# An early query bound over eight key tiles instead of four, with another order of the tasks

## The chip, the core and the metric

The kernel runs on one core of a Trainium2 chip. Five engines of that core take part: PE (TensorE: matmuls, and PEld, its weight loads), ACT (ScalarE), DVE (VectorE), POOL (GpSimd) and SP (SyncE, which here only issues DMAs). Each engine takes its instructions strictly in its own order and waits on semaphores that the others raise. The metric is the device time of the core in microseconds; lower is better. Three runs of the kernel before gave 791.34, 791.4 and 791.9 us, a median of 791.4 us.

## The reference

`x` has 2048 rows of 640 numbers in bf16. It is layer-normed once, and two branches read it: attention with 32 heads of 20 dimensions over all 2048 positions, and a two-stage MLP mixer whose result gates the attention's.

```python
def reference(A_x, A_wqkv, A_wo, B_x, B_w1, B_w2, B_w3, B_w4):
    ...
    # _A_ref: attention
    qkv = (x @ wqkv).reshape(B, S, 3, H, Dh).transpose(2, 0, 3, 1, 4)
    q, k, v = qkv[0], qkv[1], qkv[2]
    scores = jnp.einsum("bhqd,bhkd->bhqk", q, k) * (Dh ** -0.5)
    p = _softmax(scores, axis=-1)
    o = jnp.einsum("bhqk,bhkd->bhqd", p, v)
    ... @ wo
    # _B_ref: h = gelu(layernorm(x) @ w1), shifted by rows, @ w2; x1 = x + that;
    #         x1 + gelu(layernorm(x1) @ w3) @ w4
    ...
    x = A_x
    xn = _layernorm(x, axis=-1)
    s = _A_ref(xn, A_wqkv, A_wo)
    g = _silu(_B_ref(xn, B_w1, B_w2, B_w3, B_w4))
    return x + s * g
```

## The kernel before

**Tiling.** The 2048 positions are 16 key tiles of 128 and 4 query chunks of 512 (`NQC`). The 32 heads go in 8 quads of 4. For each quad and each query chunk (32 groups, named `quad_qc`, the first is `0_0`) the kernel makes, for every key tile, the scores of four heads (`sc`, lines 1615 and 1632), their exponentials, and the product with V (`pv`, line 1424). One ACT instruction (`exp`, line 1684) takes the scores of two heads of one key tile, 128 by 1024. Part of the exponentials is made by DVE from bit patterns (line 1707 and the additions of line 1594, or on POOL line 1592) for four key tiles of a group, in two blocks of two (`BLK`); these are the "units". Everything else is put between as it fits: projections of the next quads, the whole mixer branch, the output projection (all line 725).

**The shift under the exponent.** So that the exponentials stay in range, every query gets a shift computed from a bound: the largest absolute key component (`MXc[:, c]`, line 1209, one number for each of the four key chunks `c`, made from the product `KT_c`) times the sum of the absolute query components. The final bound (`mq_`, line 1226) needs all four key chunks. To start sooner, group `0_0` first uses an *early* bound, made by `early()` from the first key chunk alone (`mqe`, `she`, `qade`, lines 1178, 1184, 1188). Its queries (`qe`) serve the first `EARLY` = 4 key tiles; after these, `between()` (`fs`, `fe`) makes the factor by which the sums so far are rescaled (`rescale`), and the remaining tiles use the final bound (`sh_0`, `qad_0`, lines 1157 and 1163).

**The start.** The tiles of x come by eight DMAs of two tiles each (`ld_x`, line 912); the weights of the first quad (`ld_wp`, line 1094) and the V weights of the first half (`ld_wv0`, line 1333) come by three more on the same queue. Layer norm of the 16 tiles: for those in `LNV` DVE takes the statistics (`bn`, line 936); for those in `LNS` (tiles 1, 4, 5, 14, 15) ACT sums x and x squared (`sx`, `sxx`, lines 982 and 984). The normed tiles are transposed, by PE for chunks 0, 1 and 3 (`tr_x`, line 1071; copied out of PSUM by ACT, line 1079, or DVE, line 1082) and by DMA for chunk 2 (line 1060). Then come the products `QT_c` and `KT_c` (queries and keys of the first quad) and `v0_n` (V), each of five steps over the 640 inputs, each step four matmuls side by side. The first step of such a product waits for all five pieces of its transposed input. `kev_c` (line 1212, ACT) copies the keys out after `mx_c`.

**The order.** No engine chooses at run time: `TABLE`, a string at the end of the file, lists all 6715 tasks in one order and names the PSUM bank or buffer that each takes; `Planner.follow` reads it and derives the semaphores. The TensorE work before the first data are `NPF[0]` = 36 warm-up groups (`warm`, line 899). `AGAIN` names score matmuls that are issued more than once.

In the order of before, the starts are as follows (read from `TABLE`):

```
SP : ld_x0 ld_x2 ld_x4 ld_x6 ld_wp_1 ld_x8 ld_x12 ld_wp_0 ld_x14 ld_wv0 ld_x10 | tx_9 tx_8 ...
ACT: sx1 sxx1 sx4 sxx4 sx5 norm1 sxx5 trev_x0 (3) sx14 norm4 norm5 sxx14 qev_0 trev_x1 (5)
     sx15 kev_0 sxx15 exp (5) kev_1 trev_x3_3 exp (2) kev_2 kev_3 exp exp exp fe exp ...
PE : warm (21) tr_x0 and warm ... KT_0_0 QT_0_0 KT_0_1 QT_0_1 v0_0 (4) KT_0_2 ... she ... KT_1
```

Of the kernel before, what the change touches and what calls it, by code (L numbers as in the profile page):

```python
# [464 lines left out]
class Handle:  # L465
    _n = 0
# [11 lines left out]
class Cfg:  # L478
# [5 lines left out]
    def __init__(self, S=2048, D=640, H=32, F=1536):  # L484
# [60 lines left out]
        self.NPF = [36, 0]  # L545
# [39 lines left out]
        self.AGAIN = {(2, 2, 4, 2): 2, (7, 0, 1, 0): 1, (7, 0, 1, 1): 1, (7, 0, 8, 2): 2, (7, 1, 5, 0): 1, (7, 1, 6, 2): 1, (7, 1, 7, 3): 1, (7, 1, 9, 0): 1, (7, 1, 12, 0): 1}  # L585
        self.EARLY = 4
        self.ND = ([2, 4, 4, 4],) + tuple([5, 4, 5, 4] for _ in range(5)) + ([5, 5, 5, 5], [5, 5, 4, 4])
        self.PP |= {(quad, qc, 0, 2) for quad in range(8) for qc in range(4)}
        self.PP |= {(0, 0, 1, 3), (0, 0, 1, 2)}


    def order(self, quad, qc):
# [4 lines left out]
        first = 0 if quad + qc else 1  # L597
# [51 lines left out]
class Gen:  # L649
# [196 lines left out]
    def alloc_persistent(self):  # L846
# [44 lines left out]
        for k in range(cfg.NPF[0]):  # L891
            T("pe", 427 if k < 14 else 216, self.warm, reads=[A("Ob")], writes=[("PV", 0)], name=f"warm{k}")
# [204 lines left out]
    def prep(self):  # L1097
# [74 lines left out]
        def early():  # L1172
            e0 = self.e4[:, :]
            T("pool", 250, lambda e: e.memset(QE[:, 1536:1664], 0.0), writes=[A("mqe")], name="mqe0")
            for k in range(2):
                T("pool", 250, lambda e, k=k: e.tensor_scalar(sel[:, k, :, :], bass.AP(e0.tensor, e0.offset, [list(e0.ap[0]), [1, 4], [0, 32]]), 2.0 * k - 1.0, None,
                                                              op0=ALU.mult), reads=[A("e4")], writes=[A("sel", k)], name=f"sel{k}")
            T("dve", 90, lambda e: e.tensor_scalar(mqe[:, :, 20], self.maskn[:, 0:4], MXc[:, 0:1], None, op0=ALU.mult),
              reads=[A("MXc", 0), A("maskn"), A("mqe")], writes=[A("mqe")], name="mqe", lock=True)
# [22 lines left out]
        for c in range(NQC):  # L1202
            if c == 1:
                early()
# [929 lines left out]
    r"#9#6#:#;#<#=#>#?#@#A#B#C###_#p#,$O#(#{#`#a$P$d#-#)$8#%#&#'#*#.#$#+#j#k#i#4#D#l#u&V$N#q&W#m#E#F#G#H#I#J#n#t#r$R#v#s$Q#2#w$S#o#b$$#g$W$T#x#K#c#}#|#L$##M#N$p%$u"  # L2134
    r"'#O#P%(#$U#~$%#z#Q#R#S#T#U$&$X$Y$Z$V#y#V#W#X$z)${$|#e$}%)%*%+#Y$v%#$$]$[$~%,$/$+$,$'%$%%$-$q%&$^#Z$w$x#[$r$s$*#h#f$_&U$y$e%'$t$0$`#]#^#d%k)%d(%l%e&X#$a$b&Y&Z"
    r"&[%m%f%2$$c%g%7'%n$(%h$E$)%r%<&%3$f&]%i%=$.%>$H$1$=$2%o$3%-%%8%4%5%9%.%/%6$G%0&g(&h%?&i%1%@$C#0&`$%:&j&a&b&c%A%&d%B$<$9$6$7$:%p%;$>$;%u%j$?$4%C%D&n&&o$I&^%v#"
    r"$D&e&k$F$@%w%E$5$J&p&q&r$A&s&{$%x%&l$g%q%y&|%z%{&}&~'#*.#*?&*@'*/$%|'%('&'''($h'$#/$K$B$i$j',$*A%%G$M$k')'-$l*0''*'.$L$m*<&*=''/$n&:($o*8#*9$'0'1*>)&;&<%}*C&"
    r"*D'&=%O$*:#&>*E(%~%J&%P%K%T'%U&?*B%V%L%Q%R%S%W%M%Y#%Z%[%X%]%^%_(%`%a%b%F%H%I&#)&$%t'2(K&m%s&%&&%c*5%%N*G'*F(*6$&*$*H$&+&'&,&-&.'?#&L%'@&M(L&(&/'A*7)&)&0(M&1&"
    r"2'B'C'D(N'+*1#*2$&6)&N&O&P*3&&C#&D&7*O&*L#*N%*M$*P%&Q*b)*Q*a(*;&E&F&G&8&*c#*4&H+(%+'$&9&@+)'*T(*U)*W*Y'*Z&*I'M&*[&'N'O'P'Q*J*S$*R%&A$'R&u%&v*]&*^'&B&w&x#5'i'"
    r"h&3&y+2#*V)+3$'3('4'5'6'7*X*_$&z*e&+4(*d'*k#+$(+%)*j$'8*`'9(':';'<'=*m*f)*o'*n&+&&*g*p$'>*r$*q#*K(P+T'E&_*s*i)*h('F('G'H+6&+5'&I'I'J'K*l%+*+D)+C(+<$&R+=#*v'Y"  # L2140
    r"('Z'[+7#'L']'^'S#'T'_+E)+>&+8+/)+.(+9&+#'U+0(*|'V'W+:%+X$+;%+W#+,('X++)'a#'b+Z'c'd'e'f+K%+J&+_#+-$+^$+?&J#+G(+L#+H)*w*t+a+U%+l$+V&+m#&K+o+I%*~*y*x+Y&(O,&','("
    r"&S$&T+M,('+1+r#+s$,*%,)&*u*}+['+](,+$+u'j$'k+x+@%,E#(T&t+A&+`#,D$+B%'l'm'n*{,F('o*z'p#+F+d(+c)+N+e),7&,6%'q'r+g#,9+f$'s+b+p(+q)'t+O'u,,,4%,5&+h%,<#,=$,?+t#,8"
    r"$'`2h+~+{+i+j'+k('v$&4'w'x+n&,B&,:#,A%,;$'y'z'|#'}'~,C)(#,R%,>%'{,I(,H),Q&,T($(%,J'+z,@,o$,p#,q$,%(U,K)-&,W&(&,L(,X%,Z,$(',M#+w,k$,h',l#,G,#+y,m%,i&+v+}-4(-5"
    r")(Q&,[(R(S(e,j)-6&-)&,w%(^(V(z-*',v$,x(/y+|,n,-)-,,.(,U'-/&-0%,0$,1#,/),],N,2%,V(+P,Y#,d-2'g()$(*(+,3,r#,s$,y%,z&,f,t),^(,,e(-,a,_-=#,{%->$,P',O(,u,c-(%-'&(."
# [128 lines left out]
```

## Time and profile before

| what | us |
|---|---|
| median of the runs | 791.4 |
| the profiled execution | 791.33 |
| its span on the core | 789.6 |
| ACT busy | 760.5 |
| PE busy (pipelined, an upper bound) | 774.8 |
| DVE busy | 704.1 |
| POOL busy | 441.7 |
| first exponential starts | 22.41 |
| ACT runs without a gap from | 36.13 |
| last exponential ends | 782.6 |

The span is the time from the core's first instruction to its last; 1.7 us lie around it. Rows of the profile name a line of the kernel, the engine, the operation and its shapes, a count, busy time and the mean length in ns, and after the bar the idle time of the engine just before and what ended it. A timeline row has the start, the length and what ran; a row with x5 is five instructions without a gap. Lengths of pipelined instructions overlap: the next may start before the last one's end.

### The profile page before, as it was taken

To read this page: it belongs to the slowest core of one execution; us is meant where nothing else is said; L and a number is where in the kernel's file an instruction comes from. 1 tells how busy PE (TensorE), PEld (TensorE's weight loads), DVE (VectorE), ACT (ScalarE), POOL (GpSimd) and SP (SyncE) were. 2 spreads that over 40 slices of the span, in tenths; PEclk is the share of its full clock that TensorE was granted. 3 is DMA by queue.
4 is the path that set the end of the run, shared out by engine and by line. 5 is a ranking of instruction groups with operands and counts; after the bars stand their busy time and mean duration, and the time that the engine had idled before them with its cause. 6 is when DMAs were issued, how large, how long until landed. Compare 5 with 4: busy or idle time off the path is not lost.

```text
span 789.6 us, 27717 instructions
## 1 busy us (share of the span) xinstructions
PE 774.8 (98%) x12461; PEld 294.0 (37%) x12461; DVE 704.1 (89%) x936; ACT 760.5 (96%) x791; POOL 441.7 (56%) x238
## 2 busy tenths in 40 slices
PE   9999999999999999999999999999999999999997
PEld 5432333334434333333433333333334333333454
DVE  8888889889999999989998889898989899897987
ACT  7999999999999999999999999999999999999896
POOL 5666556562556647665564654656544546536733
PEclk9999999999999999999999999999999999999999
DMA  5332433253111233524233222234331123114343
GB/s 174 48 99 87 102 87 100 57 132 68 39 36 37 47 71 70 85 55 94 54 74 74 43 75 48 61 70 77 74 96 29 36 43 87 20 17 136 93 145 102
DMA packets 141349, 58.09 MB, mean 74 GB/s; under 512 B 113728, under 2 KB 136432, under 8 KB 141232
## 3 DMA queue, kind: packets, MB, share of 16 engines
q1 hardware_dynamic: 141232, 56.33, 30.8%
q8 instruction: 97, 1.59, 0.9%
q14 instruction: 20, 0.16, 0.1%
HBM read 34.70 MB, written 10.33 MB: 57 GB/s over the span
## 4 chain that ended last, share of the span: by engine, by line
PE 67%; ACT 26%; DVE 6%; issue 0%
PE psum L725 23%; ACT arena L1684 22%; PE psum L1615 19%; PE psum L1606 12%; PE psum L1424 8%; DVE arena L1707 3%; PE psum L899 1%; ACT arena L2090 1%; PE psum L1632 1%; ACT arena L1998 1%; PE psum L1481 1%; ACT arena L1661 1%; ACT arena L2118 1%; DVE arena L1594 1%; PE psum L1455 1%; PE psum L1071 0%
## 5 line engine op out<-in xcount | busy, mean ns | idle before, releaser
L1684 ACT ACTIVATE arena<-psum 128x1024 bf16<-128x1024 f32 x718 | 671.6, 1041 | 17.0 <-PE psum L1615 12.6
L1592 POOL TENSOR_TENSOR arena<-arena 128x2048 int32<-128x2048 int32 x92 | 330.1, 3599 | 207.8 <-DVE arena L1594 91.7
L1707 DVE TENSOR_SCALAR arena<-psum 128x1024 uint16<-128x1024 f32 x276 | 335.6, 1221 | 47.9 <-PE psum L1615 44.4
L725 PE MATMUL psum<-arena 128*32 128x320 bf16 (+1 forms) x5808 | 335.0, 333 | 0.2
L1615 PE MATMUL psum<-arena 32*128 32x512 bf16 x1935 | 257.7, 384 | 6.5 <-ACT arena L1684 2.7
L1606 PE MATMUL psum<-arena 128*22 128x512 bf16 x2208 | 193.0, 381 | 0.3 <-DVE arena L1594 0.3
L725 PEld LDWEIGHTS psum<-arena 128*32 128x32 bf16 x5808 | 137.4, 96 | 120.4 <-issue 50.6
L1615 PEld LDWEIGHTS psum<-arena 32*128 32x128 bf16 x1935 | 69.2, 91 | 227.8 <-ACT arena L1684 133.4
L1594 DVE TENSOR_SCALAR arena<-arena 128x4096 uint16<-128x4096 uint16 (+1 forms) x139 | 141.4, 1038 | 1.7 <-PE psum L1606 0.8
L1424 PE MATMUL psum<-arena 128*22 128x512 bf16 x1432 | 135.2, 382 | 0.0
L1606 PEld LDWEIGHTS psum<-arena 128*22 128x22 bf16 x2208 | 49.5, 90 | 65.8 <-issue 43.7
L1741 POOL TENSOR_TENSOR arena<-arena 128x512 bf16<-128x512 f32 x30 | 40.7, 1355 | 41.7 <-DVE arena L1594 26.7
L1424 PEld LDWEIGHTS psum<-arena 128*22 128x22 bf16 x1432 | 34.0, 90 | 49.2 <-issue 28.6
L2083 DVE CAST arena<-psum 128x512 bf16<-128x512 f32 x48 | 32.8, 685 | 4.8 <-PE psum L725 4.5
L1291 DVE CAST arena<-psum 128x512 bf16<-128x512 f32 x40 | 27.1, 685 | 2.9 <-PE psum L725 2.6
L1906 POOL TENSOR_TENSOR arena<-arena 128x640 bf16<-128x640 bf16 x12 | 17.1, 1436 | 21.1 <-DVE arena L1840 9.0
L936 DVE BATCH_NORM_STATS2 arena<-arena 128x6 f32<-128x320 bf16 x54 | 24.7, 477 | 1.6 <-POOL arena L980 1.4
L1661 ACT ACTIVATE arena<-psum 128x2048 bf16<-128x2048 f32 x13 | 24.6, 1889 | 0.7 <-PE psum L1615 0.6
L953 POOL TENSOR_SCALAR arena<-arena 128x640 bf16<-128x640 bf16 x16 | 13.9, 875 | 19.2 <-DVE arena L1594 14.2
L1632 PE MATMUL psum<-arena 128*32 128x512 bf16 x240 | 23.4, 381 | 0.1
L1728 DVE STREAM_TRANSPOSE arena<-psum 128x512 f32<-128x512 f32 x30 | 21.3, 712 | 1.6 <-PE psum L1606 1.0
L1840 DVE SCALAR_TENSOR_TENSOR arena<-psum,arena 128x320 bf16<-128x320 f32 x32 | 15.3, 488 | 6.8 <-PE psum L725 6.3
(135 smaller groups left out, 338.1 us busy)
## 6 DMA issues: line engine op xcount, KB each, us to landing
arena<-in_B_w_dram SPq DMA_DIRECT2D x48, 160.0 KB, 2.8
arena<-arena SPq DMA_DIRECT2D x124, 32.0 KB, 1.9
arena<-in_B_w_dram SPq DMA_DIRECT2D x4, 960.0 KB, 5.3
arena<-in_A_x_dram SPq DMA_DIRECT2D x8, 320.0 KB, 5.6
arena<-in_A_x_dram SPq DMA_DIRECT2D x16, 160.0 KB, 2.6
out_dram<-arena SPq DMA_DIRECT2D x16, 160.0 KB, 1.8
heads<-arena SPq DMA_DIRECT2D x120, 20.0 KB, 2.0
arena<-keys SPq DMA_DIRECT2D x28, 80.0 KB
```

The lines of the kernel that those rows point to most:

```text
L725: ins = e.matmul(pb[32 * c:32 * c + 32, 0:N], lhsT(k, c), rhs(k, c), start=(k == 0), stop=(stop and k == nk - 1), tile_position=(0, 32 * c))
L1424: ins = e.matmul(pb[32 * i:32 * i + 22, 0:512], VA[:, ql, kts[i // 2], i, :], PT[:, slots[i // 2][0].slot, slots[i // 2][0].at(i % 2):slot ...
L1592: return e.tensor_tensor(dst.bitcast(I32), U[:, ub, 0:w].bitcast(I32), bass.AP(c.tensor, c.offset, [list(c.ap[0]), [0, w // 2]]), op=ALU.add)
L1594: fa if onp else lambda e, v=v, dst=dst: e.tensor_scalar(dst, U[:, ub, 0:w], EXP_B[v], None, op0=ALU.add),
L1606: ins = e.matmul(pb[32 * i:32 * i + 22, 0:512], wv, dst[:, at:at + 512].bitcast(BF16), start=first, stop=final, tile_position=(0, 32 * i))
L1615: return e.matmul(out, self.KT[32 * i:32 * i + 32, b, 128 * kt:128 * kt + 128], q, start=True, stop=True, tile_position=(32 * i, 0))
L1632: ins = e.matmul(out[32 * c:32 * c + 32, :], self.KT[:, b, 128 * kt + 32 * c:128 * kt + 32 * c + 32], self.QM[:, gb, i, :], start=True, st ...
L1661: lambda e: e.activation(self.PT[:, hp[0].slot:hp[0].slot + 2, :], self.psum[:, 512 * h0.slot:512 * h0.slot + 2048].rearrange("p (a b) -> ...
L1684: lambda e: e.activation(self.PT[:, hp.slot, :].rearrange("p (a b) -> p a b", b=512), self.banks(hs), AF.Exp, scale=cfg.scale),
L1707: return e.tensor_scalar(U[:, ub, 1024 * at:1024 * at + 1024].rearrange("p (a b) -> p a b", b=512), self.banks(hd), a_exp, EXP_BIAS, op0=A ...
L1741: return e.tensor_tensor(OnT.rearrange("p (k d a) -> p a k d", k=4, a=4), Ob[:, :].rearrange("p (a k d) -> p a k d", a=4, k=4), in1, op=AL ...
L2083: T("dve", c_dve(512), lambda e, h=h, fc=fc, i=i, G=G: e.tensor_copy(G[:, i, fc, :], self.wbank(h)[:, 0:512]), reads=[wa], writes=at, name ...
```

## The change

- `EARLY` goes from 4 to 8: in group `0_0` the first eight key tiles (0 to 7) use the early bound. `early()` is now built after `KT_1` instead of `KT_0`, and a new DVE instruction (`mqm`) with a changed `mqe` takes the larger of the first two chunks' maxima.
- With it the two blocks that DVE serves in `0_0` become tiles (10, 11) and (14, 15) instead of (6, 7) and (10, 11); the POOL additions of that unit stay two.
- Tiles 14 and 15 move from `LNS` to `LNV`: DVE takes their statistics, and four ACT instructions (`sx14`, `sxx14`, `sx15`, `sxx15`) go. POOL applies the norm to them in both versions.
- Four warm-up groups fewer. `AGAIN` has 22 repeats instead of 11.
- `TABLE` is another: another order on all engines, above all in the first 60 us, and other PSUM banks.

```diff
-        self.NPF = [36, 0]
+        self.NPF = [32, 0]
...
-        self.AGAIN = {(2, 2, 4, 2): 2, (7, 0, 1, 0): 1, (7, 0, 1, 1): 1, (7, 0, 8, 2): 2, (7, 1, 5, 0): 1, (7, 1, 6, 2): 1, (7, 1, 7, 3): 1, (7, 1, 9, 0): 1, (7, 1, 12, 0): 1}
-        self.EARLY = 4
+        self.AGAIN = {(0, 1, 2, 2): 1, (0, 1, 5, 3): 1, (0, 1, 6, 2): 1, (5, 2, 2, 0): 1, (5, 2, 2, 1): 1, (6, 2, 12, 3): 1, (7, 0, 1, 2): 3, (7, 1, 2, 0): 2, (7, 1, 2, 1): 2, (7, 1, 6, 0): 1, (7, 1, 6, 1): 1, (7, 1, 7, 2): 2, (7, 1, 7, 3): 2, (7, 1, 8, 3): 3}
+        self.EARLY = 8
+        self.LNV = self.LNV + [[14, 15]]
+        self.LNS = [[1], [4, 5]]
...
-        self.PP |= {(0, 0, 1, 3), (0, 0, 1, 2)}
+        self.PP |= {(0, 0, 2, 3), (0, 0, 2, 2)}
...
-        first = 0 if quad + qc else 1
+        first = 0 if quad + qc else 2
...
-            T("dve", 90, lambda e: e.tensor_scalar(mqe[:, :, 20], self.maskn[:, 0:4], MXc[:, 0:1], None, op0=ALU.mult),
-              reads=[A("MXc", 0), A("maskn"), A("mqe")], writes=[A("mqe")], name="mqe", lock=True)
+            M2, m2 = self.RZ[:, 1, 0:4], A("RZ", 1)
+            T("dve", 90, lambda e: e.tensor_scalar(M2, self.maskn[:, 0:4], MXc[:, 0:1], None, op0=ALU.mult), reads=[A("MXc", 0), A("maskn")],
+              writes=[m2], name="mqm", lock=True)
+            T("dve", 90, lambda e: e.scalar_tensor_tensor(mqe[:, :, 20], self.maskn[:, 0:4], MXc[:, 1:2], M2, op0=ALU.mult, op1=ALU.min),
+              reads=[A("MXc", 1), A("maskn"), A("mqe"), m2], writes=[A("mqe")], name="mqe", lock=True)
...
         for c in range(NQC):
-            if c == 1:
+            if c == cfg.EARLY // 4:
                 early()
...
 TABLE = (
...
```

The starts in the new order:

```
SP : ld_x0 ld_x2 ld_x4 ld_x6 ld_wp_1 ld_x10 ld_x8 ld_wp_0 ld_x14 ld_x12 ld_wv0 | tx_9 tx_8 ...
ACT: sx1 sxx1 sx4 sxx4 sx5 norm1 sxx5 trev_x0 (3) norm4 norm5 qev_0 trev_x1 (5)
     kev_0 kev_1 exp (7) trev_x3_3 exp (2) kev_2 exp exp kev_3 exp ...
PE : warm (24) tr_x0 and warm ... QT_0_0 v0_0 (4) QT_0_1 QT_0_2 QT_0_3 v0_2_0 QT_0_4 v0_2 tr_x1 ...
     KT_0 (5) KT_1 (5) ... she ... sc
```

Past the first 110 of ACT's tasks its order differs from the old one only in some 25 places, by a few tasks each.

More of the change, by code (lines that the diff above doesn't have):

```diff
@@ L891, in alloc_persistent @@
         for k in range(cfg.NPF[0]):
-            T("pe", 427 if k < 14 else 216, self.warm, reads=[A("Ob")], writes=[("PV", 0)], name=f"warm{k}")
+            T("pe", (427 if k < 14 else 216) + 900 * (k == 0), self.warm, reads=[A("Ob")], writes=[("PV", 0)], name=f"warm{k}")
         self.step = 0
@@ L2237 @@
[L2237 to L2238 removed]
+    r"#6#9#:#;#<#=#>#?#@#A#B#C#D##&T#E#F#l#G#H#I#J#K#L#M#N#O#%#,#-#&#'#$#w#(#0#*#+#)#Z#g#.#f&U$X#e#[#]#h#m#i$W#P#Q#q#^#p#j#n#k$Y#r#o$Z$[#c#s#2$]$^#y#x#`#{$|(#z#|#t"
+    r"$_#u#_#}#v#~$+$a$,$4$b$c$#$)$d#R#S$`#T$r$%%#$f$}$m&#d$n$o$p$e$g#b#a$$$-$s%&$h$t$u$i$~%#$q%'$v&S%(%)$w%%$$($x(I$j#U#V$y$z#W$8$*$O${$'$k$%$A$.#X#Y$&%a'&V$&W&X&"
```

208 lines of the change are left out of this document (103 added, 105 removed).

## The prediction

> **What bounds the kernel now.** First the page: the busy time of each engine and ACT's largest group.
>
> ```profile
> span 789.6 us, 27717 instructions
> PE 774.8 (98%) x12461; PEld 294.0 (37%) x12461; DVE 704.1 (89%) x936; ACT 760.5 (96%) x791; POOL 441.7 (56%) x238
> ...
> L1684 ACT ACTIVATE arena<-psum 128x1024 bf16<-128x1024 f32 x718 | 671.6, 1041 | 17.0 <-PE psum L1615 12.6
> ```
>
> PE and ACT both look full, so the second view is the busy time by stretches, and the third the waits of ACT behind the start (36 to 782 us).
>
> ```profile
> 14.00:24.00 10.00, 9.99 (x287) 6.92 (x278) 9.81 (x39) 9.64 (x19) 5.62 (x11) 1.00 0.34 55
> 24.00:36.00 12.00, 11.99 (x254) 5.54 (x254) 9.63 (x22) 10.63 (x14) 7.17 (x10) 1.00 0.19 18
> 36.00:60.00 24.00, 23.66 (x368) 8.36 (x364) 20.96 (x29) 23.93 (x27) 17.36 (x14) 1.00 0.33 95
> ...
> ACT arena L1684 <- PE psum L1615: 11.0, 27, 0.7
> ACT arena L1684 <- PE psum L1481: 1.8, 5, 0.5
> ACT arena L1684 <- PE psum L1424: 1.2, 2, 0.8
> ```
>
> The columns of a stretch are its length, then PE, PEld, DVE, ACT, POOL busy. From 36 to 60 us ACT is busy 23.93 of 24 us while PE issues 15 matmuls per us; from 14 to 24 it issues 29. So PE has room behind the start, and ACT sets the pace there; its waits in 746 us sum to 14.6 (the three rows and 0.6 more). Before 36 us ACT waits: that is where the change acts. The timeline of ACT in that stretch:
>
> ```profile
> 13.49 0.73 ACT L982 ACTIVATE arena<-arena 128x640 bf16<-128x640 bf16 x1
> 15.89 0.72 ACT L984 ACTIVATE arena<-arena 128x640 bf16<-128x640 bf16 x1
> 16.68 0.69 ACT L1145 ACTIVATE arena<-psum,arena 128x512 bf16<-128x512 f32 x1
> 17.49 2.59 ACT L1079 ACTIVATE arena<-psum 128x512 bf16<-128x512 bf16 x5
> 21.36 0.73 ACT L984 ACTIVATE arena<-arena 128x640 bf16<-128x640 bf16 x1
> 22.41 4.69 ACT L1684 ACTIVATE arena<-psum 128x1024 bf16<-128x1024 f32 x5 [0.23 <-PE psum L1615]
> 26.95 0.81 ACT L1212 ACTIVATE arena<-psum,arena 128x512 bf16<-128x512 f32 x1
> 27.62 0.62 ACT L1079 ACTIVATE arena<-psum 128x512 bf16<-128x512 bf16 x1
> 29.07 1.94 ACT L1684 ACTIVATE arena<-psum 128x1024 bf16<-128x1024 f32 x2 [0.83 <-PE psum L1615]
> 30.90 1.45 ACT L1212 ACTIVATE arena<-psum,arena 128x512 bf16<-128x512 f32 x2
> 33.80 1.94 ACT L1684 ACTIVATE arena<-psum 128x1024 bf16<-128x1024 f32 x2 [0.55 <-PE psum L1615]
> 36.13 24.25 ACT L1684 ACTIVATE arena<-psum 128x1024 bf16<-128x1024 f32 x26
> ```
>
> The first exp starts at 22.41; from 36.13 the exps run solid, 24.25 us for 26, about 0.92 each. Whatever the change gains or loses by the point of equal work at 36.13, the rest carries to the end. In between ACT has 12.2 us of work (10 exps at 0.91, from 4.54 for five, `kev_1` 0.67, the copy 0.62, `kev_2` and `kev_3` 1.32, `fe` 0.5) and 1.5 us of waits.
>
> **The change part by part.** *Four sums less on ACT.* The row of 15.89 is followed at 16.68: 0.79 for a sum with the reading of its result, 3.1 us for the four (two more rows are those of 13.49 and 21.36), all ahead of the first exp. That is the largest gain on offer, if ACT's next instruction is ready.
>
> *It waits for another.* The new order gives x12 the tenth place of SP's queue and the V weights the last. The rows of the queue and of the two landings:
>
> ```profile
> 7.00 0.68 SPq L1333 DMA_DIRECT2D arena<-in_A_wqkv_dram  x1
> 7.73 0.94 SPq L912 DMA_DIRECT2D arena<-in_A_x_dram  x1
> ...
> arena<-in_A_wqkv_dram SPq DMA_DIRECT2D x1, 400.0 KB, 6.9
> arena<-in_A_x_dram SPq DMA_DIRECT2D x1, 320.0 KB, 7.0
> ```
>
> The tenth load lands at 7.00 + 6.9 = 13.9, the eleventh at 7.73 + 7.0 = 14.7. In the old order x10 is last and PE waits for nothing there (busy 9.99 of 10 us from 14 on). In the new one `v0_0`, which reads the V weights, stands in PE's queue between `QT_0_0` and `QT_0_1`. PE waits there until 14.8, and behind it `QT_0`, the x1 transposes, `KT_0`, `KT_1`, so `qev_0` and everything on ACT after it. (Fewer warm-ups let the first transposes go some 0.75 us earlier; this wait swallows it.) Rows for what follows:
>
> ```profile
> 9.77 1.90 PE L899 MATMUL psum<-arena 128*32 128x512 bf16 x32
> 16.78 0.39 PE L725 MATMUL psum<-arena 128*32 128x512 bf16 x3
> 18.34 0.71 PE L725 MATMUL psum<-arena 128*32 128x320 bf16 x16
> 19.52 0.39 PE L1184 MATMUL psum<-arena 128*32 128x512 bf16 x4
> 21.93 0.40 PE L1615 MATMUL psum<-arena 32*128 32x512 bf16 x4
> ...
> 10.44 1.28 DVE L936 BATCH_NORM_STATS2 arena<-arena 128x6 f32<-128x320 bf16 x3
> 17.26 0.69 DVE L1209 TENSOR_REDUCE arena<-psum 128x1 f32<-128x512 f32 x1
> 18.05 0.18 DVE L1178 TENSOR_SCALAR arena<-arena 128x4 bf16<-128x4 f32 x1
> 19.96 0.75 DVE L1188 SCALAR_TENSOR_TENSOR arena<-psum,arena 128x512 bf16<-128x512 f32 x1
> 27.23 1.42 DVE L1082 COPY arena<-psum 128x512 bf16<-128x512 bf16 x4
> 31.36 0.24 DVE L1226 TENSOR_SCALAR arena<-arena 128x4 bf16<-128x4 f32 x1
> 32.27 0.75 DVE L1163 SCALAR_TENSOR_TENSOR arena<-psum,arena 128x512 bf16<-128x512 f32 x1 [0.23 <-PE psum L1157]
> ```
>
> A step of four 512-column matmuls takes 0.217 (1.90 less 0.38 for the tail, over seven), one of 320 columns 0.137, and a product can be read 0.48 after its last step starts (16.78 to 17.26). From 14.8: `v0_0` four steps 0.55, `QT_0_1` to `_3` 0.65, `v0_2_0` 0.14, so `QT_0_4` starts at 16.14 and `qev_0` at 16.6, as before (16.68). Three more V steps and the x1 transposes put the five copies at 17.3 to 19.9 (0.5 apart, as in the row of 17.49). So ACT is where it was, with 1.55 of the four sums gone into idling.
>
> *The early bound over two chunks.* The old chain reaches `qade` from `KT_0` alone, at 19.96. The new one needs `KT_1`, whose first step waits for the last x1 copy: 20.05, five steps 1.08, readable at 21.4; `mx_1` 0.65, a small one 0.1, `mqe` 0.2, `she` after 0.15 and readable in 0.44, `qade` 0.75: 23.7; score 0.15 later, exp 0.48 after it (21.93 to 22.41): first exp at 24.35, 1.9 us later than now. `mqm` (priced as `mqe`, 0.1 to 0.2) runs while DVE waits and costs nothing. The other 1.5 us of the removed sums also become waiting; what is kept is `kev_1` done ahead (0.67).
>
> *DVE.* The two tiles add four statistics (0.4 apart in the row of 10.44) and some 0.45 of small ones, about 2.1 us. Ahead of `mx_0` they are covered: `aq_0` in DVE's queue waits for `qev_0` until 17.4, three statistics and small ones bring DVE to `mx_0` by 19.2, and `KT_0` is readable only at 19.9. Without that cover they would delay the chain one for one. Behind `qade` the norm of tiles 12 and 13 ends DVE's next 16 instructions (5.8 us by their rows' kinds) at 29.6, so the x3 transposes, and the eighth exp that PE has behind them, come at about 31.75, where ACT is free at 31.25: a wait of 0.5.
>
> *More early tiles.* Fourteen exps, not eight, go before the final bound is needed, so the two old waits (0.83 and 0.55 in the rows, 1.5 with their edges) go. Late next is the final bound itself: with the x3 copies at 30.8 instead of 27.23 `mq_` comes at 34.9 (now 31.36) and `qad_0`, 0.9 behind it and 0.75 long, ends at 36.4. The first exp on it is due at 39, but its score `sc0_0_10_1` stands in PE's queue ahead of the early `sc0_0_6_1y`, whose exp is due at 37.6 and can start at 37.45. It just fits.
>
> Sum at equal work: 24.35 + 11.55 (12.2 without `kev_1`) + 0.5 = 36.4, against 36.13: 0.3 lost.
>
> *POOL and SP past the start.* POOL's norms of tiles 14 and 15 wait for DVE's small results about as long as now; `ld_w1`, `kt0`, `qt0` and `qm0`, which change places, have their readers in later groups, and POOL is busy only 56% of the time: nothing on the path. Without that cover a late `qm0` would hold up the first group that reads it by as much as it is late. *`AGAIN`* adds 11 score matmuls, 2.4 us of PE at 0.217, at places where PE has room behind 36 us; without the room all 2.4 would count. *Four warm-ups fewer* save 0.87 us of PE ahead of data: nothing.
>
> *The rest of the order.* ACT has the same work behind the start; of its 34 waits (0.42 each) a re-ordering can remove or add a few. No row shows which; I bound it by three of them either way, 1.3 us. The scores stand in 558 runs of row matmuls instead of 566. The chain of waits shows a single pair:
>
> ```profile
> 37.41 0.32 PE psum L1615 x2
> ```
>
> This is 0.1 above a step's 0.217, so eight runs less are 0.8 us of PE. A third of it where ACT waits: 0.3 gained.
>
> Total: 791.33 (the profiled execution: span 789.6 and 1.7 around it; the median of the runs is 0.07 above) + 0.3 - 0.3 = 791.3 us. No change, by the bound of 0.2% (1.6 us), which is about what a measurement of this kernel can tell from none.
>
> **The rivals.** *It helps.* If the V weights land by 13.3, `qev_0` follows the norm of tile 5 at about 15, the last x1 copy ends at 18.4, and the first exp comes 1.4 earlier, at 22.95, where DVE's queue is the next limit. With the wait of 0.5 at the eighth exp gone too and 0.3 from the rest: 791.33 + 0.3 - 1.4 - 0.5 - 0.3 = 789.4. For it: ACT's 3.1 us are truly gone. Against: the landings came in order of issue, and total bytes are the same.
>
> *It hurts: the final bound comes late and early scores queue behind it.* Place: `sc0_0_10_1` ahead of `sc0_0_6_1y` on PE. The slack is 0.15 us; each us by which DVE's x3 copies, `KT_3`, `mx_3` or `mq_` slip further is one us of ACT. From a slip of 2 us (DVE's added 2.1 us uncovered) it decides: 791.3 + 1.85 = 793.2. For it: DVE is busy 9.81 of 10 us from 14 to 24. Against: its queue idles at `aq_0` and `mx_0` in my count.
>
> *The clock falls.* PE idles in the new start some 1.5 us for the V weights and again before `she`. The weight-load rows at the kernel's start, where each group is one of the warm-ups:
>
> ```profile
> 6.94 0.16 PEld L899 LDWEIGHTS psum<-arena 128*32 128x32 bf16 x4 [0.26 <-issue]
> 7.36 1.48 PEld L899 LDWEIGHTS psum<-arena 128*32 128x32 bf16 x28 [0.26 <-issue]
> ```
>
> Groups come 0.42 apart until 7.36 and 0.21 apart after it: PE runs at half rate for its first 5.5 us. Should it fall back in the start, which PE's issue fills, 2.75 us of matmuls are lost: 794.1. The Trainium skill ("TensorE: Matmul & The Clock Gate", Part 1) says that the clock is halved after an idle window of about 3.4 us. By that rule two shorter idles don't trigger it, and the time stays at 791.3; the rows above show the slow beginning, and none here shows a fall after it.
>
> **How the numbers follow.** No change (including that the removed work is only turned into waiting) 0.45, between 789.8 and 792.9. It helps 0.33, around 789.4 and down to 788.4 if two or three waits of ACT behind the start go as well. It hurts 0.19, around 793.2, and the clock 0.03, 794.1. Leaving out the lowest of the first and the upper ends of the others, 788.8 to 793.6 holds 8 in 10. Faster 0.33, same 0.45, slower 0.22.
>
> **What would show it.** Right: PE idle until 14.7 or so behind the first step of `QT_0`, `qev_0` near 16.6, the first exp near 24.35, ACT idling about 3 us between its x1 copies and that exp, then solid with at most one wait of 0.5 until 37. The Wv step is wrong if line 725 runs 320-column matmuls before 14; the chain is wrong if the first exp comes before 23. The forecast falls if ACT's waits behind 40 us differ from 14.6 by more than 1.6, or if ACT waits at the sixth tile for line 1163.

## The result and the profile after

| | before | after |
|---|---|---|
| median of 21 runs, us | 791.25 | 792.88 |
| lowest to highest, us | 790.61 to 792.55 | 792.10 to 795.74 |
| profiled execution, its span, us | 791.33, 789.6 | 792.68, 791.0 |

The change makes the kernel slower: the ratio of the times is 1.0024, with a 95% interval of 1.0018 to 1.0030, so 1.4 to 2.4 us. The prediction of 791.3 us and no change was wrong; its range holds the time.

The page of the kernel after, the busy times and ACT's largest group:

```profile
span 791.0 us, 27621 instructions
...
PE 775.0 (98%) x12420; PEld 292.9 (37%) x12420; DVE 706.4 (89%) x942; ACT 758.3 (96%) x783; POOL 440.8 (56%) x238
...
L1689 ACT ACTIVATE arena<-psum 128x1024 bf16<-128x1024 f32 x718 | 672.0, 1039 | 19.2 <-PE psum L1620 14.3
```

ACT has 2.2 us less to do (758.3 against 760.5), yet its exps idle 2.2 us more (19.2 against 17.0). Line numbers are two or five higher than before, by where the change adds lines: the exp of line 1684 is 1689, the scores of 1615 are 1620, the products of 725 are 727.

Busy times by stretches (the length, then PE, PEld, DVE, ACT, POOL), and ACT's waits from 36 to 782 us:

```profile
14.00:24.00 10.00, 9.84 (x268) 5.60 (x264) 9.18 (x31) 6.78 (x11) 4.27 (x11) 1.00 0.19 37
24.00:36.00 12.00, 12.00 (x264) 5.56 (x252) 10.06 (x29) 11.50 (x14) 6.60 (x10) 1.00 0.44 69
36.00:60.00 24.00, 22.97 (x354) 9.03 (x355) 19.43 (x26) 21.56 (x24) 16.77 (x15) 1.00 0.15 42
```

```profile
ACT arena L1689 <- PE psum L1620: 12.6, 32, 0.9
ACT arena L1689 <- PE psum L1486: 1.8, 4, 0.7
ACT arena L1689 <- PE psum L1429: 1.2, 2, 0.8
```

Up to 36 us the new kernel does well: from 24 to 36 ACT is busy 11.50 of 12 us, where before it was 10.63. From 36 to 60 it falls to 21.56 of 24, where before it was 23.93. The waits behind 36 us sum to 16.7 us (the three rows and 1.1 more), 2.1 above the 14.6 before. Where they lie shows in the timeline of ACT:

```profile
15.43 0.69 ACT L1147 ACTIVATE arena<-psum,arena 128x512 bf16<-128x512 f32 x1 [0.61 <-PE psum L727]
...
22.83 6.68 ACT L1689 ACTIVATE arena<-psum 128x1024 bf16<-128x1024 f32 x7 [1.28 <-PE psum L1620]
...
30.59 1.94 ACT L1689 ACTIVATE arena<-psum 128x1024 bf16<-128x1024 f32 x2 [0.48 <-PE psum L1620]
...
35.58 6.52 ACT L1689 ACTIVATE arena<-psum 128x1024 bf16<-128x1024 f32 x7
41.98 0.60 ACT L1205 ACTIVATE arena<-psum 128x512 f32<-128x512 f32 x1
43.01 2.86 ACT L1689 ACTIVATE arena<-psum 128x1024 bf16<-128x1024 f32 x3 [0.42 <-PE psum L1620]
46.37 1.94 ACT L1689 ACTIVATE arena<-psum 128x1024 bf16<-128x1024 f32 x2 [0.51 <-PE psum L1620]
48.91 3.83 ACT L1689 ACTIVATE arena<-psum 128x1024 bf16<-128x1024 f32 x4 [0.60 <-PE psum L1620]
53.22 1.94 ACT L1689 ACTIVATE arena<-psum 128x1024 bf16<-128x1024 f32 x2 [0.49 <-PE psum L1620]
55.59 7.44 ACT L1689 ACTIVATE arena<-psum 128x1024 bf16<-128x1024 f32 x8 [0.43 <-PE psum L1620]
```

Eleven exps are done by 35.58, and the 18th ends at 42.10. Before, ten were done by 36.13, at 0.93 each the 18th ended at about 43.6, and `fe`, 0.5 us, lay ahead of it, which here comes behind it, at 41.98. So at 42 us ACT is about 1.0 us ahead. Then five waits of 0.42 to 0.60, 2.45 in sum, fall between 43 and 56 us, where before there is none. The 36th exp starts at 59.34 before and at 61.02 after: the lead of 1.0 has become a lag of 1.7. At the end 1.4 of it is left.

The chain of waits says who holds ACT there: the kernel after, pieces from 37 us on.

```profile
37.52 2.75 ACT arena L1689 x3
...
40.32 0.68 PE psum L1620 x4
...
42.88 1.34 PE psum L727 x36
44.22 0.32 PE psum L1620 x2
44.54 1.19 PE psum L727 x20
...
46.31 1.74 PE psum L727 x48
...
55.02 0.55 PE psum L1620 x3
...
55.59 1.95 ACT arena L1689 x2
```

And the kernel before:

```profile
40.50 0.37 PE psum L1615 x2
...
40.89 7.45 ACT arena L1684 x8
...
48.38 0.39 PE psum L1615 x2
```

Before, ACT itself is the chain from 40.89 to 48.34. After, PE is, without a break from 40.32 to 55.57: V products and Q products (line 727), with one or two pairs of scores between them now and then. From 42 to 56 us no row of PE shows a wait (it is busy 13.82 of 14 us), while each of ACT's five waits is ended by a score of PE. ACT's early lead was scores that PE had issued ahead of these products; the products remained.

### The profile page after: what moved, and what is told of

The parts are those of the page before. It is cut to its first block, busy times and chain, and to the rows that moved or that the text cites. A ratio compares the mean times of both kernels' runs of the same rounds, so it can differ in the third digit from the quotient of the medians.

```text
span 791.0 us, 27621 instructions
## 1 busy us (share of the span) xinstructions
PE 775.0 (98%) x12420; PEld 292.9 (37%) x12420; DVE 706.4 (89%) x942; ACT 758.3 (96%) x783; POOL 440.8 (56%) x238
## 4 chain that ended last, share of the span: by engine, by line
PE 74%; ACT 19%; DVE 3%; SPq 2%; DMA 1%; issue 0%; POOL 0%; POOLq 0%
PE psum L727 27%; PE psum L1620 22%; ACT arena L1689 16%; PE psum L1611 13%; PE psum L1429 9%; ACT arena L2095 1%; PE psum L1637 1%; DVE arena L1712 1%; DMA arena<-in_A_wqkv_dram 1%; SPq L914 1%; PE psum L1486 1%; DMA heads<-arena 0%; ACT arena L2123 0%; SPq L1387 0%; PE psum L1460 0%
## 5 line engine op out<-in xcount | busy, mean ns | idle before, releaser
L1689 ACT ACTIVATE arena<-psum 128x1024 bf16<-128x1024 f32 x718 | 672.0, 1039 | 19.2 <-PE psum L1620 14.3
L727 PE MATMUL psum<-arena 128*32 128x320 bf16 (+1 forms) x5808 | 329.3, 333 | 0.7 <-DMA arena<-in_A_wqkv_dram 0.3
L1620 PE MATMUL psum<-arena 32*128 32x512 bf16 x1946 | 261.2, 384 | 6.3 <-ACT arena L1689 3.3
L727 PEld LDWEIGHTS psum<-arena 128*32 128x32 bf16 x5808 | 135.5, 96 | 121.1 <-issue 48.6
L1911 POOL TENSOR_TENSOR arena<-arena 128x640 bf16<-128x640 bf16 x12 | 16.7, 1398 | 22.0 <-DVE arena L1845 10.4
```

The lines of the kernel that those rows point to most:

```text
L727: ins = e.matmul(pb[32 * c:32 * c + 32, 0:N], lhsT(k, c), rhs(k, c), start=(k == 0), stop=(stop and k == nk - 1), tile_position=(0, 32 * c))
L1620: return e.matmul(out, self.KT[32 * i:32 * i + 32, b, 128 * kt:128 * kt + 128], q, start=True, stop=True, tile_position=(32 * i, 0))
L1689: lambda e: e.activation(self.PT[:, hp.slot, :].rearrange("p (a b) -> p a b", b=512), self.banks(hs), AF.Exp, scale=cfg.scale),
```

## The experiments

Three theories stand in the expectations. *A* is the prediction's: behind the start ACT sets the pace and PE has room, so the loss must come from the start. *P*: between about 41 and 55 us PE's queue sets the pace, so work and order on PE count there. *Q*: the masked copies of Q for the second group (`qm0_1`), which come late in the new order, hold up the first scores of that group and what stands behind them.

All results in one table. The difference is that of the medians to the kernel before on the same chip; the two columns behind it are from the profiles: the start of the first exp, and the time from the start of the 8th exp to that of the 33rd (the stretch behind the start; before 24.33). Three more kernels, with less work on PE, have their numbers in their own paragraph.

| kernel | difference, us | ratio [95%] | first exp | 8th to 33rd exp |
|---|---|---|---|---|
| after | +1.63 | 1.0024 [1.0018, 1.0030] | 22.83 | 27.72 |
| after, no repeats in the second group | +1.43 | 1.0022 [1.0013, 1.0031] | 23.05 | 27.70 |
| before, with these repeats | +0.54 | 1.0006 [0.9997, 1.0015] | 21.70 | 24.63 |
| after, PE's idle time filled | +1.78 | 1.0019 [1.0010, 1.0028] | 22.85 | 27.83 |
| after, sums of 14, 15 on ACT | +2.80 | 1.0041 [1.0028, 1.0053] | 23.46 | 27.72 |
| after, 0.68 us more of PE | +2.42 | 1.0028 [1.0017, 1.0039] | 23.09 | 28.36 |
| before, 0.68 us more of PE | +0.32 | 1.0006 [0.9997, 1.0015] | 22.16 | 24.69 |
| after, order 1, no wait for copies | +0.96 | 1.0015 [1.0006, 1.0024] | 23.53 | 27.17 |
| after, order 2 | +1.23 | 1.0019 [1.0008, 1.0030] | 23.17 | 27.02 |
| after, order 2, no wait for copies | +1.73 | 1.0024 [1.0015, 1.0033] | 24.52 | 27.02 |
| after, V weights tenth | +1.17 | 1.0015 [1.0007, 1.0024] | 22.22 | 27.71 |
| after, order 2, V weights tenth | +0.72 | 1.0007 [0.9998, 1.0016] | 23.12 | 27.02 |
| after, order 2, V weights ninth | +0.75 | 1.0008 [1.0000, 1.0017] | 23.36 | 27.02 |
| before, sums of 14, 15 on DVE | +1.75 | 1.0020 [1.0011, 1.0029] | 22.36 | 24.25 |
| before, copies of Q late | +1.71 | 1.0024 [1.0013, 1.0035] | 21.59 | 28.81 |

The 8th to 33rd of the family of before and that of after are not to be set against each other: 1.3 us of `kev_2` and `kev_3` stand ahead of the 8th exp in before and behind it in after. Within a family they compare. The stretch is read from one profile of each kernel.

**The repeats.** Three of the added repeats lie in the second group. One kernel leaves them out of after, one puts them into before.

```diff
-        self.AGAIN = {(0, 1, 2, 2): 1, (0, 1, 5, 3): 1, (0, 1, 6, 2): 1, (5, 2, 2, 0): 1, ...
+        self.AGAIN = {(5, 2, 2, 0): 1, ...
```

> The changed kernel without its three repeated score matmuls of the second group (quad 0, chunk 1). Theory P (PE issues without a gap from 14 us to the end of the second group, and sets the pace there; what the change lost between 41 and 58 us is PE's time): three steps of 0.217 = 0.65 us of PE go, the time falls by 0.4 to 0.65 us, to 792.2 to 792.5, and the exps from 56 us on come that much earlier. Theory A (that of the prediction: ACT sets the pace behind the start and PE has room): nothing moves, 792.9.

> The kernel before with the same three repeated score matmuls added and nothing else. Theory P: PE is just as full there, so 0.4 to 0.65 us more than the kernel before: 791.6 to 791.9. Theory A: PE has room behind 36 us, and the time stays at 791.25.

Without them the stretch is the same (27.70 and 27.72) and so is the time, within the intervals; the 0.4 to 0.65 us that P expected did not come. The trace shows where they went: behind their place a score waits 0.41 us for DVE (at 56.22) where in after it waits 0.19 (at 56.01). In before they add 0.30 to the stretch, half of their 0.65 us of PE, and nothing that can be measured in the time. They are not the loss.

**Filling PE's idle time.** In the new kernel PE idles from 38 to 41 us: its row there carries a wait for a bank that ACT has not read yet.

```profile
38.63 1.16 PE L1620 MATMUL psum<-arena 32*128 32x512 bf16 x6
40.32 0.68 PE L1620 MATMUL psum<-arena 32*128 32x512 bf16 x4 [0.53 <-ACT arena L1689]
```

This experiment moves products into that gap (in the lines on PE's order a score's name stands for its two heads).

```diff
 PE:
-... v0_12_0 v0_12_1 pv0_0_k6 v0_12_2 sc0_0_11_1 ... sc0_0_7_0 sc0_0_14_1 sc0_0_5_1 v0_12_3 fs ...
+... v0_12_0 v0_12_1 v0_12_2 v0_12_3 v0_12_4 pv0_0_k6 sc0_0_11_1 ... sc0_0_7_0 v0_10_0 v0_10_1 v0_10_2 sc0_0_14_1 sc0_0_5_1 v0_10_3 v0_10_4 fs ...
-... v0_15_4 sc0_0_14_0 QT_3_0 QT_3_1 QT_3_2 ...
+... v0_15_4 QT_3_0 QT_3_1 sc0_0_14_0 QT_3_2 ...
```

> The changed kernel with the V products of tiles 12 and 10 moved ahead in PE's queue, into the idle stretch at 39 to 40.6 us, tile 10 in the bank that tile 12 leaves, and QT_3 begun ahead of a pair of scores; the same instructions in all. Theory P: 0.9 to 1.2 us of PE's 1.5 us of idling are used, and the time falls by 0.6 to 1.2, to 791.7 to 792.3, although ACT gets one score some 0.2 us later at 39 us. Theory A: ACT's waits behind 41 us have other causes (banks, VectorE's results), and the time stays within 0.3 of 792.9.

PE's busy time from 36 to 42 us rises from 5.22 to 5.66 of 6, less than half of the 0.9 to 1.2 expected, and ACT's waits from 36 to 62 us stay at 2.4, in four instead of five:

```profile
ACT arena L1689 <- PE psum L1620: 2.4, 4, 1.1
```

Two waits (0.51 and 0.60) became one of 1.1 behind the moved work, and the stretch is 27.83. To do a product earlier is not enough: the scores that follow need a free bank. The second of the two pairs ahead of that wait starts at 46.04, released by an exp at 46.00, about half a us behind the first pair; in after the two pairs start together, at 45.88. P's 0.6 to 1.2 us did not come, and this run left P undecided.

**The layer norm's part undone.** The sums of tiles 14 and 15 go back to ACT, in the order of after.

```diff
-        self.LNV = self.LNV + [[14, 15]]
-        self.LNS = [[1], [4, 5]]
 ACT: ... trev_x1 (5)
-     kev_0 kev_1 exp (7) ...
+     sx14 kev_0 sxx14 kev_1 sx15 sxx15 exp (7) ...
```

> The changed kernel with the sums of tiles 14 and 15 given back to ACT, at places where ACT idles between the x1 copies and the first exp; VectorE loses its 2.1 us of statistics again. The first exp comes 0.4 to 0.8 us later (23.2 to 23.6 in place of 22.83). Theory P: ACT's lead is not used by PE, so the time stays within 0.3 of 792.9. Theory A: ACT sets the pace, and the time grows by the 0.4 to 0.8 us: 793.3 to 793.7.

It costs 1.2 us more than after does: the first exp starts 0.6 later, the x3 transposes 0.5 later again, and the stretch behind is the same to the last digit (27.72). So the four removed sums are worth about 1 us in the new order, and the loss isn't theirs. This missed what P expected (no change) and is more than A's 0.4 to 0.8: PE's queue holds the x3 transposes, these came later too (one waits 0.34 us for POOL at 30.23, which none does in after), and all of PE's work behind them moved along.

**Less work on PE.** V products of tiles 8 to 15 take 64 columns in place of 320 in four of their five steps, which leaves out a part of V: in after, in before (tiles 0 to 7), and in after with the second group's first scores not waiting for the copies.

```diff
+            w = 64 if k and name in self.THIN else N
-                    ins = e.matmul(pb[32 * c:32 * c + 32, 0:N], lhsT(k, c), rhs(k, c), ...
+                    ins = e.matmul(pb[32 * c:32 * c + 32, 0:w], lhsT(k, c), rhs(k, c)[:, 0:w], ...
```

> The changed kernel with the V products of tiles 8 to 15 cut: of their five steps the last four have 64 columns in place of 320 (a part of V is left out), some 0.08 us each, 2.5 us of PE less between 28 and 52 us, with the order as it is. Theory P (PE's own work sets the pace between 41 and 55 us: V and Q products that the new order puts there): the waits of ACT behind 43 us shrink from 2.4 to under 1 us and the time falls by 1.2 to 2 us, to 790.9 to 791.7. Theory Q (the masked copies of Q for the second group, which follow the later final bound through fe, the rescaling, a clearing of 3.5 us on POOL and four DMAs, land at 50.8 in place of 45.8 us; until then there is nothing but the first group's exps, so a lead of ACT is idled away): the time stays within 0.4 of 792.9.

> The kernel before with the same cut of the V products of tiles 8 to 15. ACT runs solid there from 36 to 60 us, so both theories expect at most 0.4 us less: 790.7 to 791.3. If it falls by more than 1 us, PE's work sets the pace of both kernels and the difference between them is not in these products.

> As the first, and besides the first scores of the second group (key tiles 0, 2, 3, 5, 6, 7 and half of 1), which run as row matmuls and read Q itself, no longer wait for the masked copies that they do not read. Theory P: as the first run within 0.3. Theory Q: with the copies out of the way the shorter PE work counts, 0.5 to 2 us less than the first run.

The ratios are 1.0021 [1.0012, 1.0030], 0.9996 [0.9988, 1.0005] and 1.0014 [1.0005, 1.0023]. The first and the third can't be read as meant, because the granted clock of PE fell in their profiles. Stretches of the first; the number behind POOL's is the granted clock:

```profile
38.00:41.90 3.90, 3.05 (x44) 1.14 (x46) 3.32 (x4) 3.90 (x5) 1.93 (x4) 1.00 0.01 2
41.90:48.70 6.80, 6.41 (x94) 2.17 (x86) 3.25 (x7) 3.70 (x6) 3.51 (x1) 0.51 0.02 4
48.70:52.00 3.30, 3.07 (x92) 1.43 (x84) 2.83 (x6) 2.79 (x4) 1.25 (x5) 0.98 0.14 37
```

With less to do PE idled a little more (5.00 of 6 us busy from 36 to 42, against 5.22), its clock was halved for 6.8 us, and what was saved was lost again. The third kernel came out 0.9 us below the first by the medians, as Q expected, but in its profile the clock was halved for 3.4 us only, so this is no sign for Q. Here the question whether PE sets the pace had to be asked by adding work, not by taking it away.

**More work on PE.** The first step of five V products is issued twice, 0.68 us of PE, in both kernels.

```diff
-                for c in range(4):
-                    ins = e.matmul(..., start=(k == 0), stop=...)
+                for z in range(r):          # r = 2 for k == 0 of v0_8, 9, 13, 14, 15
+                    for c in range(4):
+                        ins = e.matmul(..., start=(k == 0), stop=z < r - 1 or ...)
```

> The changed kernel with the first step of the V products of tiles 8, 9, 13, 14 and 15 issued twice (the second overwrites the first): five steps of 0.137 = 0.68 us more of PE between 42 and 52 us, nothing else. Theory P (PE's queue is full from 41 to 55 us and sets the pace there): 0.5 to 0.7 us more than the changed kernel, 793.4 to 793.6. Theory A (that of the prediction, PE has room behind the start): 792.9.

> The same five repeated steps in the kernel before, where they lie between 39 and 49 us and ACT is solid. Theory P, if PE is full there as well: 0.3 to 0.6 us more, 791.5 to 791.9; theory A: 791.25.

In after the stretch grows by 0.64 (28.36 against 27.72) and ACT's waits from 36 to 62 us from 2.4 to 3.1:

```profile
ACT arena L1693 <- PE psum L1624: 3.1, 5, 1.0
```

Nearly all of 0.68 counts, and the medians agree (2.42 against 1.63), though their intervals overlap. In before 0.36 counts (24.69 against 24.33) and the time stays within what can be measured. That is P: in the new kernel PE has no room there. In the old one it has some, but less than the prediction took it to have.

**Late copies of Q.** In the new kernel the factor `fe` comes at 41.98 (with twice the early tiles), `rescale` behind it, and then POOL's clearing of the copies' buffer and SP's copies. The rows of POOL and SP after:

```profile
43.43 3.51 POOL L1407 MEMSET arena<- 128x4096 bf16 x1 [3.54 <-DVE arena L1405]
...
46.97 6.75 SPq L1387 DMA_DIRECT2D arena<-arena  x8
```

Before they stand at 38.14 and 41.68, so they come 5.3 us later now. Is that a loss of its own? In after the trace says no. The last of the four copies lands at 50.78, and the first scores of the second group are the second and third pair of this row of PE, from 52.89 on:

```profile
52.77 0.73 PE L1620 MATMUL psum<-arena 32*128 32x512 bf16 x6
```

They are issued 2.1 us behind the landing, without a wait. What late copies can do was tried in before: there they wait for a late exp.

```diff
+        by["qm0_1"].preds.add(by["exp0_0_12_1"].id)
```

> The kernel before with one wait added: the four DMAs that copy Q for the second group are issued only when the exp of key tile 12 (second pair) is done, at about 46.3 in place of 41.7 us, so that they land some 4.6 us later, as in the changed kernel. Nothing else moves. Theory Q: the first score of the second group, in its place at 47.7 us, waits until about 50.4, PE behind it too, and the time grows by 2 to 3.5 us, to 793.2 to 794.7. Theory P: the copies are not what the second group waits for, 791.2 to 791.6.

```profile
48.65 0.39 PE L1617 MATMUL psum<-arena 32*128 32x512 bf16 x4 [1.39 <-DMA arena<-arena]
```

The copies land at 48.60, PE waits 1.39 for them, and the stretch grows by 4.5: 1.39 of waiting and, in this profile, a fall of the clock behind it (below). The time grows by 1.71, less than Q's 2 to 3.5. So late copies can hurt; whether they do in the new order was asked by two kernels in which the first 13 pairs of scores of the second group, those issued by rows, which read Q itself, don't wait for them:

```diff
-  reads=[...] + ([] if gb is None else [A("QM", gb)]),
+  reads=[...] + ([] if gb is None or (quad, qc, kt, a) in self.ROWS else [A("QM", gb)]),
```

Both also have another order of the tasks between 13 and 60 us (orders 1 and 2 of the table), so a third has order 2 with every wait kept; none has the three repeats. In order 2 the V and Q products on PE are spread between each other and the scores, and the products with P come elsewhere:

```diff
 PE:
-... sc0_0_8_0 v0_15_0 v0_12_4 v0_10_2 v0_10_3 v0_10_4 v0_15_1 v0_15_2 v0_15_3 v0_15_4 sc0_0_14_0 QT_3_0 QT_3_1 ...
+... sc0_0_8_0 v0_10_2 pv0_0_k5 v0_15_0 v0_10_3 v0_15_1 v0_15_2 QT_3_0 v0_10_4 v0_15_3 sc0_0_14_0 v0_15_4 QT_3_1 ...
```

> The changed kernel without its three repeats in the second group, whose first scores (key tiles 0, 2, 3, 5, 6, 7, half of 1; row matmuls that read Q itself) don't wait for the masked copies of Q, and with the order of 13 to 60 us arranged anew for that (second group's scores earlier, some V products later). Theory Q (the late copies keep the second group's scores back while ACT idles): 0.5 to 1 us less than the changed kernel, 791.9 to 792.4. If the copies are no limit: 792.5 to 793.

> The changed kernel without its three repeats in the second group and with the order of 13 to 60 us arranged anew (V and Q products spread otherwise between the scores, the second group's first scores as early as their copies of Q allow); every wait on data as it was, the same work. If the order of PE's queue is where the change lost its time (theory P): 0.4 to 0.9 us less than the changed kernel, 792.0 to 792.5. If the copies of Q (theory Q) bind, the second group's first score waits for them at 51 to 52 us and the time is 792.9 or more.

> The run before it, order and all, but the second group's first scores, row matmuls that read Q itself, don't wait for the masked copies of Q. Theory P: as the run before it within 0.2 us. Theory Q: 0.5 us or more less than that.

The time of order 1 without the wait (+0.96) fell where Q had put it, but that kernel differs from after in its order too. The last two have one order and differ in the wait alone: 27.02 us each. The copies cost nothing there, and Q is refuted for order 2 as well; with every wait kept they land at 51.90, and the first scores that wait for them start behind 52.38. The order alone takes 0.70 off the stretch (27.72 to 27.02; the missing repeats have no part in it, by the first experiment), and ACT's waits from 36 to 62 us go from 2.4 to 1.5, in both:

```profile
ACT arena L1689 <- PE psum L1620: 1.5, 4, 0.5
```

That the kernel without the wait was slower in time (1.0024 against 1.0019, by more than P's 0.2 us) lies within the intervals. Its profile shows something else, by chance: there the V weights, issued at 7.58, landed at 14.7, a microsecond later than in after. The load's row, PE's and ACT's:

```profile
arena<-in_A_wqkv_dram SPq DMA_DIRECT2D x1, 400.0 KB, 7.1
```

```profile
14.84 1.81 PE L727 MATMUL psum<-arena 128*32 128x320 bf16 x36 [2.17 <-ACT arena L1022]
...
24.52 1.94 ACT L1691 ACTIVATE arena<-psum 128x1024 bf16<-128x1024 f32 x2 [1.30 <-PE psum L1620]
```

The profile puts PE's 2.17 down to ACT's norm, which ended at 14.72. But with order 2 and every wait kept PE starts the same row at 13.76, while that norm ends at 14.96: it was the load. This is the case that the prediction had worked out (14.8 and 24.35).

**V weights earlier.** The V weights go to the tenth place of SP's queue, ahead of x12: in after, and in order 2. In order 2 they also go to the ninth.

```diff
-SP : ... ld_wp_0 ld_x14 ld_x12 ld_wv0 | ...
+SP : ... ld_wp_0 ld_x14 ld_wv0 ld_x12 | ...
```

> The changed kernel with the load of the V weights one place earlier in SP's queue, tenth in place of eleventh, ahead of x12; nothing else. If the V weights hold up the start (they land at 13.6 us and the first V step waits 0.3 to 0.5 us for them), they land at some 12.8, the first exp comes 0.3 us earlier and the time is 792.5. If x12, now last, is needed as soon (VectorE's statistics of its tiles at 15 to 25 us), or the start waits for something else, 792.7 to 793.

> The changed kernel with both mendings: no repeats in the second group and the order of 13 to 60 us arranged anew (alone 0.5 to 0.7 us), and the V weights tenth in SP's queue of loads (alone 0.6 to 0.7 us). If these are two separate causes, one at the start and one in PE's queue behind 41 us, they add up: 1.1 to 1.4 us less than the changed kernel, 791.5 to 791.8, and what stays of the loss is under 0.5 us. If the earlier start is lost again behind 41 us, 792.2.

> The same with the V weights ninth, ahead of x14 too. If PE still waits for them in tenth place, up to 0.3 us less than the run before it; if not (the first V step no longer waits at 12.8 us there), the same within 0.2, or up to 0.5 more where VectorE's statistics of tiles 14 and 15 now come late.

In after the weights land at 12.69, PE no longer waits for them, and the first exp starts at 22.22:

```profile
22.22 6.68 ACT L1689 ACTIVATE arena<-psum 128x1024 bf16<-128x1024 f32 x7 [1.28 <-PE psum L1620]
```

The stretch behind is unchanged (27.71). By the ratios the earlier weights take the loss from 1.9 us (0.24% of 791) to 1.2, the order alone to 1.5, and both together to 0.55, with an interval that reaches no change. Each of these has an interval of 0.7 us or more to either side, so the parts are rough; the two together account for most of the loss. What the earlier weights add to order 2 is not shown by the profiles: with their landing at 12.28 the first exp starts at 23.12, with it at 13.63 at 23.17; in the first case the last of the x1 transposes waits 0.48 us, and the profile doesn't show for what. That gain rests on the medians alone. The ninth place gives nothing beyond the tenth. No version that does all of the work was faster than the kernel before.

**The layer norm's part alone.** In before, tiles 14 and 15 go to DVE, with the start's order fitted to that and the early bound left at four tiles.

```diff
         self.EARLY = 4
+        self.LNV = self.LNV + [[14, 15]]
+        self.LNS = [[1], [4, 5]]
```

> The kernel before with one part of the change alone: the sums of tiles 14 and 15 on VectorE; early bound over four tiles, warm-ups and repeats as before, the order of the first 60 us arranged anew around the moved sums. As the prediction has it (VectorE's added 2.1 us are covered, the four sums only become waiting): 790.9 to 791.6. If VectorE has no cover ahead of the first exp and the x3 transposes, its 2.1 us show up for the most part: 792 to 793.

```profile
22.36 1.94 ACT L1686 ACTIVATE arena<-psum 128x1024 bf16<-128x1024 f32 x2 [2.03 <-PE psum L1617]
```

The first exp starts where it did (22.41 before), and most of the time of the removed sums stands as a wait of 2.03 in front of it. The time is 1.75 us longer, as expected for DVE's work without cover, but not by the way expected, for the first exp is no later. The profiled execution, the fastest of the eleven, shows 0.25 us by the 33rd exp and 0.85 at the last one; where the rest lies stays open. The early bound over eight tiles was not run alone, so which part of the change calls for which part of the new order stays open too.

## Why the prediction was wrong

**The premise on PE: the step that failed.** "So PE has room behind the start, and ACT sets the pace there." That was read from the number of matmuls per us (15 against 29). It does not show room, for the matmuls are not the same. Of the 287 from 14 to 24 us, 80 are transposes of 128 columns, started about 0.02 us apart, and 6 are scores by rows; of the 368 from 36 to 60 us none is such a transpose and 68 are scores by rows, about 0.13 us each, and PE is busy nearly without a gap. In the chains, two scores by rows take 0.32 to 0.39, one column step 0.217. The Trainium skill ("TensorEngine Tiling (Array Packing)", Key Properties) says that changing the tiling mode drains TensorE; the rows agree, with 0.1 us or more on top of a step for each such pair of scores. Two things were drawn from the premise. One is that a lead of ACT at equal work is kept to the end; the lead of 1.0 us was given back within 14 us. The other is "I bound it by three of them either way, 1.3 us" for the rest of the order, which stands in the sum as 0.3 gained: it cost 2.45 us in five waits, and 2.1 over all waits behind 36 us. The prediction's own sign of failure, waits that differ from 14.6 by more than 1.6, came true. The profile before held the warning: PE was 23.66 of 24 us busy from 36 to 60 us, and the chain of waits there, apart from one piece of ACT's, is PE's.

**The landing of the V weights: a term mis-sized.** "The eleventh at 7.73 + 7.0 = 14.7." After's rows of the load (issued at 7.65) and of PE:

```profile
arena<-in_A_wqkv_dram SPq DMA_DIRECT2D x1, 400.0 KB, 6.0
```

```profile
13.65 2.00 PE L727 MATMUL psum<-arena 128*32 128x320 bf16 x44 [0.31 <-DMA arena<-in_A_wqkv_dram]
```

It landed at 13.6, and PE waited 0.31 for it, not until 14.8; 320-column matmuls before 14 were the prediction's own sign that this step is off. `qev_0` came at 15.43 (predicted 16.6) and the first exp at 22.83 (24.35). The mechanism was right: over the profiles with the V weights last, the landing ran from 13.6 to 14.7 and the first exp from 22.83 to 24.52, 9.0 to 9.8 behind it. One row of one execution had been taken for a fixed time. The first exp came 1.5 earlier than foreseen, 1.1 of it by the landing, and equal work, foreseen 0.3 late, came 1.0 early.

**What the two make together.** 791.33 less 1.0 (equal work) plus 2.45 (the five waits) plus 0.25 (a remainder, put down to the overlap of neighbouring exps that is lost at each wait), less 0.3 given back by the end: 792.7; the profiled execution took 792.68. Two errors of opposite sign stand behind the 1.4 us between this and 791.3: equal work came 1.3 us better than the sum had it, and the rest 2.7 us worse. That the time stayed within the range is luck.

**The chain over two chunks: right in length.** From the first step of `KT_1` (18.73) to the first exp (22.83) it took 4.1 us; predicted were 4.3 (20.05 to 24.35). The sign set for it, a first exp before 23, came true by the earlier landing and not by a shorter chain. `kev_1` went ahead of the first exp as foreseen.

**The eighth exp and the final bound: right.** The wait of 0.5 stands in the row of 30.59 (0.48). The final bound just fits: the seven exps from 35.58 run without a gap.

**DVE's 2.1 us: right in this order only.** With the early bound over two chunks the added statistics are covered, and the removed sums are worth about 1 us (the run with the sums back on ACT). Put into before, with an order fitted to it, the same edit costs 1.75.

**POOL, SP, repeats, warm-ups.** `qm0` did come late, by 5.3 us, without being what binds: right in the sum, though its cover was thinner than said, as 1.39 us of PE's waiting in before with late copies shows. The three repeats of the second group cost nothing that can be measured: right; the others were not tried. The reason given for them, room on PE, is wrong for after.

**The rivals.** *It helps* had the start right (first exp 22.95) and the end wrong, for it rested on the same premise; the landing at 13.6 missed its condition, 13.3. *It hurts* had about the right time, 793.2, by another mechanism: the final bound was not late. *The clock falls* did not happen in the profiled execution (granted clock 1.00 in the rows of 14 to 60 us). It happens in some of the runs: in 5 of the 21 runs of after the granted clock averaged 0.997 or less over the run, and their median is 794.33 against 792.72 for the others; of 156 runs of before 2 show it.

## What to carry to other kernels

An engine that is busy without a gap may have little room or none, however few instructions it issues; ask what one more of its instructions would cost, and add some to see. A lead won by issuing the urgent work first is a loan when the same engine still owes the rest: follow the chain of waits until both kernels have done the same work on every engine, not on the pacing one alone. A transfer's landing is a spread, not a number: price what hangs on it at both ends.

## What the runs showed of the hardware

The clock was halved after less idling than the prediction took. In before with late copies, PE idled for 1.39 us until 48.65. Stretches of that kernel, the granted clock behind POOL's busy time:

```profile
46.00:50.00 4.00, 2.62 (x46) 1.05 (x43) 1.52 (x3) 3.25 (x4) 4.00 (x3) 1.00 0.39 87
50.00:57.00 7.00, 6.77 (x52) 1.18 (x50) 4.58 (x6) 4.29 (x5) 3.52 (x2) 0.52 0.65 224
57.00:61.00 4.00, 4.00 (x58) 1.17 (x54) 3.31 (x4) 3.52 (x4) 1.01 (x3) 0.99 0.00 0
```

The clock is 0.52 from 50 to 57 us, some 3 us after the gap began, and full again behind it; 52 matmuls are issued in these 7 us, and 58 in the 4 us after. In the kernel with thin V products several short gaps went before the fall, none above 0.53 us: PE was busy 3.05 of the 3.90 us up to 41.9, then the clock was 0.51 for 6.8 us. The Trainium skill ("TensorE: Matmul & The Clock Gate", Part 1) puts the halving after at least one idle window of about 3.4 us; here no gap was half as long. The same page (A second HAM failure mode: psum-queue depth-cycling) tells of frequent micro-idles that make the clock swing, and that agrees with the rows of the thin V products. The prediction weighed the first rule and not the second.

The busy share of PE alone does not say when the clock falls. A stretch of the kernel before that is thinner than that of the thin V products (5.00 of 6 us from 36 to 42) kept its clock:

```profile
702.00:708.00 6.00, 4.86 (x66) 1.42 (x54) 5.95 (x8) 6.00 (x7) 0.00 (x0) 1.00 0.26 38
```

In order 2 with the V weights ninth the clock was halved from 725.7 to 729.1 us, where PE had been busy 2.96 of the 3.40 us before. What decides stays open, and so does where it fell in the runs of after that show a lower clock.

The landing of the last of eleven loads at the start differs by 1.1 us between executions of kernels that load in the same order (13.60 to 14.71), and the first exp with it: about as much as the 1.0 us of lead that the new start had won.
